# The low 16-bit step of a weight narrowing, moved from VectorE to GpSimd from tile 26 on

## The chip, the core and the metric

The kernel runs on one core of one Trainium2 chip. A core has five engines that each work through a fixed order of their own: TensorE (PE in the profile; its weight loads are PEld), VectorE (DVE), ScalarE (ACT), GpSimd (POOL) and SyncE (SP), which issues most DMA transfers. GpSimd issues some transfers too. The metric is the device time of one execution in microseconds (us), taken as the median of several runs. Of the kernel before three runs were timed: 965.84, 966.92 and 969.87 us, so the median is 966.92. A separate execution was profiled.

## The reference

Three layers follow each other. The inputs of attention are float32; the weights of the two layers behind it are float64 arrays:

```python
# 1. attention: q, k, v are (4 batches, 8 heads, 576, 64)
q_rot, k_rot = rotate(q), rotate(k)          # x1*cos - x2*sin, x1*sin + x2*cos on the two halves of 64
scores = q_rot @ k_rot.T / sqrt(64)
attn = exp(scores - max(scores)); attn /= sum(attn) + 1e-9
x = (attn @ v) as 2304 tokens x 512
# 2. moe1: w1, w2, w3 are 512x768, w_out is 768x512
h = max(x @ w1, x @ w2, x @ w3);   x = h @ w_out
# 3. moe2: w_in is 512x2048, w_out is 2048x512
h = x @ w_in;   g = h / (1 + exp(-h));   return g @ w_out     # 2304 tokens x 512, float32
```

All of it is computed in one launch.

## The kernel before

**Tiles and stages.** Attention goes batch by batch and, in a batch, by pairs of heads. A pair is cut into tiles of query rows. For each tile TensorE makes the scores (L440 and L443), VectorE takes the negated maximum (L453, output `nb`), ScalarE takes the exponential (L460, output `e`), VectorE the reciprocal of the sums (L470), and ScalarE normalises (L472). The result is moved through four DMA transfers (L511, `pt<-e`) into another layout, transposed in place by VectorE (L533, `pt<-pt`), and multiplied with v on TensorE (L574 and L578, output `xp`). VectorE or ScalarE evacuates that product (L582, L581). Between these steps TensorE works on moe1 of the batch before (L673, outputs `m`), whose results VectorE and ScalarE combine (L704, L711, L702, L727). The function `attention()` yields once per tile, and the tile's number is `j`.

**Ropes.** q and k of a pair of heads are loaded by SP into a raw buffer `qk` (L305, two transfers each for q and for k, and L308 for the last 64 rows). For batches after the first, the rotation (the rope) is done wholly by GpSimd: three instructions (L366, L367, L370) on the q half (128x512 elements), the same three on the k half (128x512), and the same three on the rest (128x128). The fourth instruction of a rope is thus the first that needs k.

**The narrowing.** The weights of moe2 lie in DRAM with 64-bit elements and are narrowed on chip to 32 bits by `narrow_w2`, in 64 pieces of 128x256, first 32 of `moe2_w_in` ("wi"), then 32 of `moe2_w_out` ("wo"). Each step `n` of that generator issues work for several pieces at once:

- the load of piece `n` into a buffer `z64` (four of them in turn): by SP for wi, by GpSimd's queue for wo (both L869)
- the cast of piece `n-2` on ScalarE, from the upper 32-bit word of each element into a buffer `z` (L229; `narrow_a` with `low=False`)
- the low step of piece `n-3` on VectorE: it writes the third 16-bit word of each element of `z64` from the second (L241; `narrow_low`)
- the second and third step of piece `n-3` on VectorE: shift and mask of `z` (L248), and the merge of `z64` into `z` (L249), which reads what the low step wrote; both are in `narrow_b`
- the measure of piece `n-5` on ScalarE (L155), and its store to a scratch in DRAM (by SP, L844, for wi; by GpSimd's queue, L849, for wo), from which it comes back later (`za<-zwi`, L976) to be summed by GpSimd (L982)

So the work on a piece is: load, cast (ScalarE), low step, second step, third step (VectorE), measure and store. A piece's `z64` is free for a new load when its third step is done.

**What sets the order.** The program is written as generators that are advanced tile by tile, and a scheduler turns it into one fixed order per engine by a simulation of the timeline; `tc.issue_after(x)` holds an instruction back until `x` has been placed. The low, second and third step are held behind the last maximum, the cast behind the last exponential. On the chip each engine takes its instructions in its fixed order and waits on semaphores for what they need.

**Where tile 26 is.** `LOOSE` is 25, and `attention()` sets `b_now[0]` to 1 for `j > LOOSE`, so from tile 26 on. The narrowing's first L248 of all starts at 176.1 us in the trace, the last third step at 535.5.

Of the kernel before, what the change touches and what calls it, by code (L numbers as in the profile page):

```python
# [12 lines left out]
ALU = mybir.AluOpType  # L13
# [9 lines left out]
def fused_kernel(  # L23
# [22 lines left out]
    nc = tc.nc  # L46
# [66 lines left out]
    ps_am, b_now = [], [0]  # L113
# [69 lines left out]
    class Weights:  # L183
# [50 lines left out]
                else:  # L234
                    nc.scalar.activation(out=q[:, :, 2], in_=q[:, :, 1], func=AF.Copy, scale=step, bias=off)

        def narrow_low(self, r):
            if r is None:
                return
            q = r.bitcast(U16).rearrange("p (n t) -> p n t", t=4)  # L240
            nc.vector.tensor_scalar(out=q[:, :, 2], in0=q[:, :, 1], scalar1=2.0 ** -13, scalar2=2.0 ** -15 - 0.5, op0=ALU.mult, op1=ALU.add)  # L241

        def narrow_b(self, i, r):
            if r is None:
# [586 lines left out]
    def narrow_w2(W, src, nm):  # L831

        part = {}
        M = W.m * 512 // 256
        for n in range(M + 5):
            if n >= 5:
                W.measure(n - 5)
                if nm == "wi":  # L840
                    i, o = divmod(n - 5, 2)
                    q, c = divmod(i, KC)
                    half, f = divmod(4 * q + 2 * o, HB)
                    nc.sync.dma_start(  # L844
                        out=zscr[nm].rearrange("p (f c a i n) -> p f c a i n", c=2, a=2, i=2, n=P)[:, f:f + 2, c % 2, c // 2, half],
                        in_=W.t[n - 5].rearrange("p (f n) -> p f n", n=P),
                    )
                else:
                    nc.gpsimd.dma_start(out=zscr[nm][:, (n - 5) * 256:(n - 4) * 256], in_=W.t[n - 5])  # L849
            if 3 <= n <= M + 2:  # L850
                with tc.issue_after(last["max"]):
                    W.narrow_low(part.get(n - 3))
                    W.narrow_b(n - 3, part.pop(n - 3, None))
            if 2 <= n <= M + 1:
                if wide:
                    W.t[n - 2] = z_p.tile([P, 256], F32, tag="z", name="z")
                with tc.issue_after(exps[-1]):
                    W.narrow_a(n - 2, part.get(n - 2), low=False)
            if n < M:
                i, o = divmod(n * 256, 512)  # L860
                if nm == "wi":
                    q, c = divmod(i, KC)
                    from_ = src[c * P:(c + 1) * P, q * 512 + o:q * 512 + o + 256]
                else:
                    from_ = src[i * P:(i + 1) * P, o:o + 256]
                if wide:
                    part[n] = z64_p.tile([P, 256], w1.dtype, tag="z64", name="z64")
                    with tc.issue_after(last["load"]) if nm == "wi" else nullcontext():
                        (nc.sync if nm == "wi" else nc.gpsimd).dma_start(out=part[n], in_=from_)  # L869
                else:  # L870
                    W.t[n] = z_p.tile([P, 256], F32, tag="z", name="z")
                    nc.sync.dma_start(out=W.t[n], in_=from_)
            yield
        t = W.scale_a(n=M)
        yield
        with tc.issue_after(last["score"]):
            W.scale_b("s" + nm, t)
        yield
# [464 lines left out]
    def narrow_all():  # L1343
        yield from narrow_w2(WI, wi2, "wi")
        yield from narrow_w2(WO, wo2, "wo")
# [118 lines left out]
```

## Time and profile before

| | us |
|---|---|
| median of three runs | 966.92 |
| profiled execution | 963.49 |
| its span | 961.7 |

| engine | busy us | share of the span |
|---|---|---|
| TensorE (PE) | 898.0 | 93% |
| its weight loads (PEld) | 666.2 | |
| VectorE (DVE) | 708.4 | 74% |
| ScalarE (ACT) | 608.4 | 63% |
| GpSimd (POOL) | 479.4 | 50% |

The span runs from the first to the last recorded instruction; 1.79 us of the execution lie around it. Busy shares are averages over stages with different limits. Idle time of an engine that is not the bottleneck costs nothing by itself, so for a change the question is which wait ends last in the stage that it touches.

### The profile page before, as it was taken

The page shows a single profiled execution, that of the slowest core. Times are in us where ns is not written, and L with a number is a line of the kernel's source. Part 1 is how long each engine was busy: PE and PEld are TensorE (multiplying, and loading weights), DVE is VectorE, ACT ScalarE, POOL GpSimd, SP SyncE. Part 2 cuts the span into 40 slices and gives each one's busy share as a digit, 9 for nine tenths or more (in the row PEclk, how much of TensorE's full clock was granted, in tenths as well). Part 3 has the DMA queues.
Part 4 walks back from the last instruction along what each step waited for, and adds up shares of the span by engine and source line. Part 5 has one row for each costly group of instructions (what it writes and reads, how often), then busy time and mean ns, then how long its engine had stood idle before and what let it go on. Part 6 is the DMA issues. An engine that isn't in the chain of part 4 may idle for free.

```text
span 961.7 us, 19066 instructions
## 1 busy us (share of the span) xinstructions
PE 898.0 (93%) x6802; PEld 666.2 (69%) x6802; DVE 708.4 (74%) x1271; ACT 608.4 (63%) x1405; POOL 479.4 (50%) x546
## 2 busy tenths in 40 slices
PE   2787998999999999999998999999998999999997
PEld 1453665656666666556655787788887888888886
DVE  6769887877788677889888577365786767766554
ACT  1988678758788677798888445453553545545342
POOL 6744585870326503543443066355485466463363
PEclk9688999999999999999999999999999999999999
DMA  6953034968899976899987852364443443423201
GB/s 153 288 148 109 14 105 124 190 122 190 184 193 202 215 140 148 228 232 230 264 232 207 211 184 88 115 198 132 132 150 102 135 157 102 138 84 131 62 1 45
DMA packets 173679, 146.30 MB, mean 152 GB/s; under 512 B 50960, under 2 KB 156176, under 8 KB 173584
## 3 DMA queue, kind: packets, MB, share of 16 engines
q1 hardware_dynamic: 167984, 131.77, 54.8%
q0 software_dynamic: 4096, 12.59, 4.2%
q8 instruction: 54, 0.88, 0.4%
q10 hardware_dynamic: 1504, 0.72, 0.3%
q14 instruction: 41, 0.34, 0.1%
HBM read 90.51 MB, written 26.21 MB: 121 GB/s over the span
## 4 chain that ended last, share of the span: by engine, by line
PE 50%; DMA 10%; DVE 9%; ACT 6%; SPq 5%; issue 4%; POOL 2%; DVEq 0%; ACTq 0%; POOLq 0%
PE m L673 9%; PE m L1114 8%; PE mb L1114 6%; DMA pt<-e 6%; PE c L1177 4%; PE a L1177 4%; PE b L1177 4%; SPq L511 3%; PE mg L673 3%; PE s L443 2%; PE xp L578 2%; PE d L1177 2%; POOL gsum L1061 2%; ACT e L472 2%; ACT e L460 1%
## 5 line engine op out<-in xcount | busy, mean ns | idle before, releaser
L673 PEld LDWEIGHTS <-w 128*128 128x128 f16 x1632 | 159.4, 98 | 59.7 <-issue 16.2
L673 PE MATMUL m<-x,w 128*128 128x256 f16 (+1 forms) x1348 | 185.3, 287 | 9.8 <-DVE t L704 4.6
L1177 PEld LDWEIGHTS <-g 128*128 128x128 f16 x1485 | 146.1, 98 | 17.7
L1114 PEld LDWEIGHTS <-w8s 128*128 128x128 f16 x1344 | 131.1, 98 | 16.1 <-issue 0.9
L460 ACT ACTIVATE e<-s,nb 128x576 f32<-128x576 f32 x144 | 105.3, 737 | 33.9 <-DVE nb L453 26.7
L453 DVE TENSOR_REDUCE nb<-s 128x2 f32<-128x1152 f32 (+1 forms) x80 | 98.4, 1231 | 32.0 <-PE s L443 26.8
L472 ACT ACTIVATE e<-e,rec 128x576 f32<-128x576 f32 x144 | 103.9, 765 | 9.4 <-DVE rec L470 8.9
L366 POOL TENSOR_TENSOR w<-qk,sin_sb 128x512 f32<-128x512 f32 (+2 forms) x40 | 42.4, 1060 | 115.1 <-DMA qk<-in_q_dram 100.4
L443 PE MATMUL s<-T 64*128 64x512 f32 x256 | 78.7, 685 | 0.0
L578 PE MATMUL xp<-pt,vd 128*64 128x256 f32 (+1 forms) x512 | 77.0, 417 | 0.2 <-DVE pt L533 0.2
L533 DVE STREAM_TRANSPOSE pt<-pt 128x1024 f32<-128x1024 f32 (+1 forms) x60 | 67.6, 1128 | 11.4 <-DMA pt<-e 11.4
L1128 POOL TENSOR_TENSOR z<-t 128x256 f32<-128x256 f32 x32 | 27.1, 847 | 89.6 <-DVE t L1120 53.9
L1066 DVE SCALAR_TENSOR_TENSOR g<-gsum,sg,g 128x1024 f16<-128x1024 f32 x36 | 49.1, 1371 | 22.1 <-ACT g L1065 21.7
L1065 ACT ACTIVATE g<-gsum,sg 128x1024 f16<-128x1024 f32 x36 | 40.8, 1141 | 37.1 <-POOL gsum L1061 37.1
L673 PE MATMUL m<-h,wo 128*128 128x256 f16 (+1 forms) x448 | 62.1, 286 | 0.4 <-POOL wo L175 0.3
L673 PEld LDWEIGHTS <-wo 128*128 128x128 f16 x512 | 49.6, 98 | 15.7 <-issue 2.0
L578 PEld LDWEIGHTS xp<-pt,vd 128*64 128x64 f32 x512 | 35.4, 137 | 33.6 <-issue 12.1
L1177 PE MATMUL c<-w,g 128*128 128x256 f16 x376 | 48.9, 277 | 0.0
L367 POOL TENSOR_TENSOR qk<-qk,cos_sb 128x512 f32<-128x512 f32 (+2 forms) x44 | 47.3, 1079 | 2.8
L1177 PE MATMUL b<-w,g 128*128 128x256 f16 x376 | 48.5, 273 | 0.0
L1177 PE MATMUL a<-w,g 128*128 128x256 f16 x376 | 47.9, 273 | 0.0
L955 POOL TENSOR_TENSOR z<-z 128x256 f32<-128x256 f32 x32 | 30.4, 978 | 32.0 <-DMA z<-zwo 26.2
(268 smaller groups left out, 1999.8 us busy)
## 6 DMA issues: line engine op xcount, KB each, us to landing
w8s<-w8scr SPq DMA_DIRECT2D x64, 448.0 KB, 4.4
pt<-e SPq DMA_DIRECT2D x192, 128.0 KB, 4.4
z<-in_moe_w_in_dram SPq DMA_DIRECT2D x32, 256.0 KB, 3.8
z<-in_moe_w_out_dram POOLq DMA_DIRECT2D x32, 256.0 KB, 4.4
w8scr<-w8o SPq DMA_DIRECT2D x32, 256.0 KB, 3.7
w<-in_moe_w_dram SPq DMA_DIRECT2D x6, 768.0 KB, 5.3
wo<-in_moe_w_dram SPq DMA_DIRECT2D x6, 768.0 KB, 4.9
qk<-in_q_dram SPq DMA_DIRECT2D x32, 128.0 KB, 3.5
```

The costliest lines, as they stand in the source:

```text
L366: tt(out=w4, in0=t4, in1=sin2, op=ALU.mult)
L367: tt(out=t4, in0=t4, in1=cos2, op=ALU.mult)
L443: last["s"] = last["score"] = nc.tensor.matmul(s[:, o:o + 512], qs[r], kt[r], start=True, stop=True).ins
L453: x = nc.vector.tensor_reduce(out=nb[:, 0:m], in_=both(s, 0, 960, 576) if m > 1 else s[:, 0:576], op=ALU.max, axis=AX.X, negate=True)
L460: x = nc.scalar.activation(out=e[:, HK[g]], in_=s[:, SK[g]], func=AF.Exp, bias=nb[:, g:g + 1], accum_out=sm[:, g:g + 1])
L472: nc.scalar.activation(out=e[:, HK[g]], in_=e[:, HK[g]], func=AF.Copy, scale=r[:, g:g + 1])
L533: nc.vector.transpose(out=x, in_=x)
L578: nc.tensor.matmul(xp[r, 0:n], v4[:, g, c, :], turned(c, g), start=False, stop=(c == 3))
L673: x = nc.tensor.matmul(ps[:, 0:n], l, r, start=(first and i == 0), stop=(not more and i == len(passes) - 1))
L1066: nc.vector.scalar_tensor_tensor(out=l, in0=x, scalar=sg_t[jb], in1=h, op0=ALU.mult, op1=ALU.subtract)
L1114: nc.tensor.matmul(o, l, r, start=(i == 0), stop=(i == len(passes) - 1))
L1177: x = nc.tensor.matmul(ps, l, r, start=first, stop=last_, skip_group_check=True)
```

## The change

The low step gets its engine as an argument. A small function `low(i, eng)` issues the low step of piece `i` once, and remembers it in the set `lows`. From tile 26 on (`b_now[0]` set), step `n` issues the low step of piece `n-2` on GpSimd, right behind ScalarE's cast of the same piece. Where it has not been issued by then, the low step of piece `n-3` is issued on VectorE ahead of the second step, as before. All else is written as it was.

```diff
-        def narrow_low(self, r):
+        def narrow_low(self, r, eng):
             if r is None:
                 return
             q = r.bitcast(U16).rearrange("p (n t) -> p n t", t=4)
-            nc.vector.tensor_scalar(out=q[:, :, 2], in0=q[:, :, 1], scalar1=2.0 ** -13, scalar2=2.0 ** -15 - 0.5, op0=ALU.mult, op1=ALU.add)
+            eng.tensor_scalar(out=q[:, :, 2], in0=q[:, :, 1], scalar1=2.0 ** -13, scalar2=2.0 ** -15 - 0.5, op0=ALU.mult, op1=ALU.add)
...
-        part = {}
+        part, lows = {}, set()
         M = W.m * 512 // 256
+
+        def low(i, eng):
+            if i not in lows:
+                lows.add(i)
+                W.narrow_low(part.get(i), eng)
+
         for n in range(M + 5):
...
             if 3 <= n <= M + 2:
                 with tc.issue_after(last["max"]):
-                    W.narrow_low(part.get(n - 3))
+                    low(n - 3, nc.vector)
                     W.narrow_b(n - 3, part.pop(n - 3, None))
...
                 with tc.issue_after(exps[-1]):
                     W.narrow_a(n - 2, part.get(n - 2), low=False)
+                if b_now[0]:
+                    low(n - 2, nc.gpsimd)
```

In the orders of the built programs, 59 of the 64 low steps stand on GpSimd and five (pieces 0 to 4) on VectorE. The number of instructions on TensorE and ScalarE is the same. From tile 26 on the scheduler's order also differs in other places. In the new program the lines behind the change have other numbers: L844, L849, L869, L976 and L982 of before are L850, L855, L877, L984 and L990. Pieces count from 0; the buffer z64_0_2974 (z64_0_2973 before) holds piece 20, z64_1_3067 piece 21, and so on up to z64_2_3405 (z64_2_3404 before) with piece 26 and z64_3_3506 with piece 27.

First place: GpSimd's order at the rope on the raw buffer qk_0_3739 (before). In the rows a name left of the arrow is written, those right of it are read.

```order
L366 TENSOR_TENSOR w_0_4063<-qk_0_3739,sin_sb_0_120 128x512
L367 TENSOR_TENSOR qk_0_3739<-qk_0_3739,cos_sb_0_119 128x512
L370 TENSOR_TENSOR qk_0_3739<-qk_0_3739,w_0_4063 128x512
L366 TENSOR_TENSOR w_0_4063<-qk_0_3739,sin_sb_0_120 128x512
L367 TENSOR_TENSOR qk_0_3739<-qk_0_3739,cos_sb_0_119 128x512
L370 TENSOR_TENSOR qk_0_3739<-qk_0_3739,w_0_4063 128x512
L366 TENSOR_TENSOR w_0_4063<-qk_0_3739,sin_sb_0_120 128x128
L367 TENSOR_TENSOR qk_0_3739<-qk_0_3739,cos_sb_0_119 128x128
L370 TENSOR_TENSOR qk_0_3739<-qk_0_3739,w_0_4063 128x128
```

And the same place now, from the rope's fourth instruction on; the raw buffer is called qk_0_3740.

```order
L366 TENSOR_TENSOR w_0_4063<-qk_0_3740,sin_sb_0_120 128x512
L241 TENSOR_SCALAR z64_0_2974<-z64_0_2974 128x256
L367 TENSOR_TENSOR qk_0_3740<-qk_0_3740,cos_sb_0_119 128x512
L370 TENSOR_TENSOR qk_0_3740<-qk_0_3740,w_0_4063 128x512
L366 TENSOR_TENSOR w_0_4063<-qk_0_3740,sin_sb_0_120 128x128
L367 TENSOR_TENSOR qk_0_3740<-qk_0_3740,cos_sb_0_119 128x128
L370 TENSOR_TENSOR qk_0_3740<-qk_0_3740,w_0_4063 128x128
L241 TENSOR_SCALAR z64_1_3067<-z64_1_3067 128x256
L241 TENSOR_SCALAR z64_2_3127<-z64_2_3127 128x256
```

The low step of piece 20 now stands behind the rope's fourth instruction, and those of pieces 21 and 22 behind the whole rope.

SP's order at the loads of that rope, before: q, then k in two transfers with the move of a tile (pt) between them.

```order
L305 DMA qk_0_3739<-in_q_dram 128x4x64 x2
L308 DMA qk_0_3739<-in_q_dram 64x2x64
L869 DMA z64_2_3126<-in_moe2_w_in_dram 128x256
L844 DMA zwi_0_137<-z_2_2971 128x2x128
L305 DMA qk_0_3739<-in_k_dram 128x4x64
L511 DMA pt_1_3107<-e_1_3024 32x8x128 x4
L305 DMA qk_0_3739<-in_k_dram 128x4x64
```

And now.

```order
L305 DMA qk_0_3740<-in_q_dram 128x4x64 x2
L308 DMA qk_0_3740<-in_q_dram 64x2x64
L877 DMA z64_2_3127<-in_moe2_w_in_dram 128x256
L850 DMA zwi_0_137<-z_2_2971 128x2x128
L305 DMA qk_0_3740<-in_k_dram 128x4x64 x2
L511 DMA pt_1_3108<-e_1_3025 32x8x128 x4
```

The second k load has moved ahead of the four pt transfers.

VectorE's order at the same place now: the third steps of pieces 20 and 21 (L249) and what stands behind them up to the maximum of the next tile.

```order
L249 SCALAR_TENSOR_TENSOR z_0_3124<-z64_0_2974,z_0_3124 128x256
L470 RECIPROCAL rec_3_3312<-rec_3_3312 128x1
L704 SCALAR_TENSOR_TENSOR t_0_3277<-m_1_3264,t_5_3262 128x256
L249 SCALAR_TENSOR_TENSOR z_1_3234<-z64_1_3067,z_1_3234 128x256
L124 TENSOR_REDUCE amax_1_3327<-tr_0_3325 1x1
L582 SCALAR_TENSOR_TENSOR x_0_2096<-xp_0_3300,vs_1_1815,x_0_2096 128x320
L453 TENSOR_REDUCE nb_0_3293<-s_0_3289 128x2
```

Each third step now waits for GpSimd; behind that of piece 21 stand a reduction of one row, an evacuation and the maximum.

Second place: GpSimd's order at the rope on qk_2_4163, which had no other work between its nine instructions before. Now:

```order
L241 TENSOR_SCALAR z64_1_3337<-z64_1_3337 128x256
L366 TENSOR_TENSOR w_0_4560<-qk_2_4163,sin_sb_0_120 128x512
L367 TENSOR_TENSOR qk_2_4163<-qk_2_4163,cos_sb_0_119 128x512
L370 TENSOR_TENSOR qk_2_4163<-qk_2_4163,w_0_4560 128x512
L366 TENSOR_TENSOR w_0_4560<-qk_2_4163,sin_sb_0_120 128x512
L241 TENSOR_SCALAR z64_2_3405<-z64_2_3405 128x256
L241 TENSOR_SCALAR z64_3_3506<-z64_3_3506 128x256
```

The low steps of pieces 26 and 27 stand behind the fourth instruction of this rope, the first that reads k.

VectorE's order at the third step of piece 26, before.

```order
L241 TENSOR_SCALAR z64_2_3404<-z64_2_3404 128x256
L248 TENSOR_SCALAR z_2_3589<-z_2_3589 128x256
L470 RECIPROCAL rec_3_3632<-rec_3_3632 128x2
L249 SCALAR_TENSOR_TENSOR z_2_3589<-z64_2_3404,z_2_3589 128x256
L453 TENSOR_REDUCE nb_0_3625<-s_0_3621 128x2
L533 STREAM_TRANSPOSE pt_0_3377<-pt_0_3377 128x1024
```

And now.

```order
L248 TENSOR_SCALAR z_2_3589<-z_2_3589 128x256
L470 RECIPROCAL rec_3_3633<-rec_3_3633 128x2
L249 SCALAR_TENSOR_TENSOR z_2_3589<-z64_2_3405,z_2_3589 128x256
L453 TENSOR_REDUCE nb_0_3626<-s_0_3622 128x2
L533 STREAM_TRANSPOSE pt_0_3378<-pt_0_3378 128x1024
```

The maximum and the transpose stand right behind the third step as before; the low step has left VectorE.

SP's order at the loads of this rope, now.

```order
L305 DMA qk_2_4163<-in_q_dram 128x4x64 x2
L308 DMA qk_2_4163<-in_q_dram 64x2x64
L305 DMA qk_2_4163<-in_k_dram 128x4x64
L511 DMA pt_1_3576<-e_0_3461 32x8x128 x4
L305 DMA qk_2_4163<-in_k_dram 128x4x64
```

Before, these rows stand in the same sequence, and the second k load is transfer 302 of SP's order in both programs, with the same 301 transfers ahead of it.

## Rows read from the trace of the kernel before

**Rows 1.** busy time by stretch: start:end, us, then per engine, TensorE clock, DMA

```profile
280.00:330.00 50.00, 49.63 (x346) 32.04 (x346) 39.74 (x80) 39.55 (x118) 32.60 (x37) 1.00 1.01 206
...
sum 370.00, PE 356.57 PEld 229.43 DVE 298.31 ACT 287.03 POOL 149.69; mean PE 118.86 PEld 76.48 DVE 99.44 ACT 95.68 POOL 49.90
```

**Rows 2.** waits, 175 to 540 us: total us, times, longest

```profile
POOL w L366 <- DMA qk<-in_q_dram: 100.4, 4, 43.6
DVE nb L453 <- PE s L443: 20.1, 16, 3.2
...
PE s L440 <- ACT e L460: 4.7, 7, 1.2
...
PE s L433 <- ACT e L460: 2.1, 3, 1.2
```

**Rows 3.** VectorE groups by form: busy us, mean ns | idle before

```profile
L249 DVE SCALAR_TENSOR_TENSOR z<-z,z 128x256 int32<-128x256 int32 x64 | 34.4, 537 | 0.4
L241 DVE TENSOR_SCALAR z<-z 128x256 uint16<-128x256 uint16 x64 | 30.2, 472 | 0.0
L248 DVE TENSOR_SCALAR z<-z 128x256 int32<-128x256 int32 x64 | 27.2, 425 | 0.0
```

**Rows 4.** VectorE's timeline, 284 to 291 us: start, us, instruction [idle before]

```profile
284.37 0.40 DVE L249 SCALAR_TENSOR_TENSOR z<-z,z 128x256 int32<-128x256 int32 x1
...
287.31 1.34 DVE L453 TENSOR_REDUCE nb<-s 128x2 f32<-128x1152 f32 x1
...
289.74 0.44 DVE L241 TENSOR_SCALAR z<-z 128x256 uint16<-128x256 uint16 x1
289.98 0.31 DVE L248 TENSOR_SCALAR z<-z 128x256 int32<-128x256 int32 x1
```

**Rows 5.** GpSimd groups by form, the same operation on wider tiles

```profile
L233 POOL TENSOR_SCALAR wo<-wo 128x768 uint16<-128x768 uint16 x6 | 12.4, 2069 | 4.6 <-ACT w L229 3.4 <-ACT rec L469 0.9
...
L233 POOL TENSOR_SCALAR w<-w 128x512 uint16<-128x512 uint16 x5 | 7.5, 1492 | 4.3 <-ACT wo L229 4.0
```

**Rows 6.** instructions of L248 and L249: least/median/most ns, first to last

```profile
L248 DVE TENSOR_SCALAR z<-z x64: 304/317/1353, 176.1 to 534.6; 128x256 int32<-128x256 int32 x64
...
L249 DVE SCALAR_TENSOR_TENSOR z<-z,z x64: 400/422/1471, 177.5 to 535.5; 128x256 int32<-128x256 int32 x64
```

**Rows 7.** GpSimd's timeline, 281 to 321 us

```profile
281.74 1.54 POOL L370 TENSOR_TENSOR qk<-qk,w 128x512 f32<-128x512 f32 x1
285.83 1.27 POOL L366 TENSOR_TENSOR w<-qk,sin_sb 128x512 f32<-128x512 f32 x1 [2.56 <-DMA zwi<-z]
...
291.47 0.46 POOL L370 TENSOR_TENSOR qk<-qk,w 128x128 f32<-128x128 f32 x1
...
320.35 1.27 POOL L366 TENSOR_TENSOR w<-qk,sin_sb 128x512 f32<-128x512 f32 x1 [0.45 <-POOL qk L370]
```

**Rows 8.** SP's timeline, loads of k

```profile
277.89 0.55 SPq L305 DMA_DIRECT2D qk<-in_k_dram  x1
...
281.63 0.61 SPq L305 DMA_DIRECT2D qk<-in_k_dram  x1
...
316.27 0.62 SPq L305 DMA_DIRECT2D qk<-in_k_dram  x1
```

**Rows 9.** TensorE's timeline at 290 us

```profile
290.30 0.49 PE L440 MATMUL s<-kd,T 128*128 128x128 f32 x2 [0.37 <-ACT e L460]
```

**Rows 10.** VectorE's timeline, 309 to 313 us

```profile
309.48 0.55 DVE L249 SCALAR_TENSOR_TENSOR z<-z,z 128x256 int32<-128x256 int32 x1
310.82 1.36 DVE L453 TENSOR_REDUCE nb<-s 128x2 f32<-128x1152 f32 x1 [0.78 <-PE s L443]
312.09 1.24 DVE L533 STREAM_TRANSPOSE pt<-pt 128x1024 f32<-128x1024 f32 x1
```

**Rows 11.** TensorE's timeline, 315 to 317 us

```profile
315.33 1.08 PE L578 MATMUL xp<-pt,vd 128*64 128x256 f32 x8
316.34 0.49 PE L440 MATMUL s<-kd,T 128*128 128x128 f32 x2
```

## The prediction

> **What bounds the kernel now.** The change acts from tile 26 to the last narrowed piece, 175 to 545 us, so I read busy time by stretch first [rows 1]. TensorE is busy for 356.57 of these 370 us: no more than 13.4 us can be won there, since nothing is taken from TensorE. From 280 to 330 it is idle for 0.37 us: in that stretch any wait that reaches it is lost time. VectorE is busy for 298.31 us and GpSimd for 149.69. Then the waits [rows 2]: VectorE's maximum waits 20.1 us for TensorE's scores, in 16 tiles, while TensorE waits only 4.7 and 2.1 us, in ten tiles, for the exponentials that stand behind that maximum. So TensorE leads and VectorE mostly follows close behind. GpSimd's ropes wait 100.4 us in just four waits for a q that has not landed. That row matters most: an instruction put behind such a rope in GpSimd's order comes late, and in the kernel before nothing with a deadline stands there.
>
> **What goes from VectorE.** 59 of the 64 low steps (the first five are issued before tile 26 and stay). Their mean is 472 ns [rows 3], 27.8 us in all. But the queue doesn't hold that long: the low step that began at 289.74 is followed at 289.98 [rows 4]. A step takes 0.24 us of VectorE's queue, 59 x 0.24 = 14.2 us.
>
> **What GpSimd takes on.** No row shows this step at 256 elements there. The same operation with the same stride took 1492 ns at 512 and 2069 ns at 768 elements [rows 5]; the line through both gives 0.92 at 256. Bounds: half of the first, 0.75, and the first itself, 1.49. I take 0.9, on the line: 53 us on an engine with 220 us free. As busy time it fits.
>
> **What the two engines do to each other.** VectorE's second step has a median of 317 ns and a maximum of 1353, its third 422 and 1471 [rows 6]; the means are 425 and 537 [rows 3]. I put this excess, 64 x (0.108 + 0.115) = 14.3 us, wholly down to GpSimd working beside, the most it can be: 0.096 us for each of its 149.7 us, and 5 us for 53 more. That leaves 14.2 - 5 = 9 us, 0.15 us per piece. The Trainium skill ("SBUF — State Buffer", section "Who interferes with whom") has a cause for such outliers: the two engines share a port pair, which one of them holds for its whole instruction against some kinds of VectorE operation. The trace agrees so far that both steps come out over 0.9 us longer at worst. Another page ("Perfetto Trace Analysis", "Optimizing Scalar/DVE Operations") warns that moving work between just these two might not help; by it the relief below would be 0 instead of -1.5 and the sum +10.5 instead of +9.
>
> **Relief on the path.** It counts only where TensorE waits for an exponential: ten gaps [rows 2] by one step each, 10 x 0.15 = 1.5 us. Bounds: 0, and 4.7 + 2.1 = 6.8 if every such wait goes. I take -1.5, since a step of 0.24 us is small beside gaps of 0.7.
>
> **The wait that is added.** The third step of a piece, on VectorE, now waits for GpSimd, and behind it on VectorE stand evictions, the reciprocal, the next maximum and the transpose that feeds TensorE's products with v. So each low step has a deadline: the start of the third step in the trace of before. Where GpSimd is idle, 0.9 us fits between cast and deadline. It doesn't at the ropes between 279 and 329 us. Pieces count from 0.
>
> First place, pieces 20 and 21. In the old trace the rope on qk_0_3739 ends its third step at 281.74 + 1.54 = 283.28 and waits for its k half until 285.83 [rows 7], whose second load was issued at 281.63 behind four pt transfers [rows 8]. In the new order that load is next to the first, issued at 277.89: it lands before 283.3, and the fourth step can start at once, 2.5 us earlier. With piece 20 between, the rope ends not at 291.47 + 0.46 = 291.9 [rows 7] but at 291.9 - 2.5 + 0.9 = 290.3. Piece 21 stands behind it and ends at 291.2; VectorE wanted it at 284.37 [rows 4]. Behind it come a short reduction, one evacuation and the maximum: about 292.4 where it was 287.31 [rows 4], 5.1 us late. Slack behind that is none: the scores of 290.30 had waited 0.37 us for the exponential [rows 9]. I'd charge 4.5 us for this place alone.
>
> Second place, piece 26. It stands behind the fourth step of the rope on qk_2_4163, which began at 320.35 [rows 7]. This step needs the second k load, issued at 316.27 [rows 8]. That load has the same place behind the same four pt transfers in SP's order in both programs, and the same transfers before it, so I see nothing that lets it land earlier. The fourth step (1.27) and piece 26 (0.9) then end at 322.5. VectorE wanted the piece at 309.48, and right behind stand the maximum (310.82) and the transpose (312.09) [rows 10]. The third step of 0.55 goes first, so the maximum starts near 323.1, 12.3 us late, and the transpose ends at 312.09 + 1.24 + 12.3 = 325.6. TensorE's products that need it began at 315.33, with the next scores behind them at 316.34 [rows 11]: 325.6 - 315.3 = 10.3 us late, less what TensorE can do meanwhile. Its order is fixed, and between the two scores it keeps the same work, so I take 10.
>
> The two places don't add: a shift of 4.5 us at the first moves VectorE's deadline at the second, while the landing of the load is held by SP's order. So 10 covers both, unless the shift holds up SP as well: the pt transfers ahead of the load need exponentials, and then the charge is 10 + 4.5 = 14.5. From below it is 0: GpSimd could be early, if that load comes well before 316.27, or TensorE could have work that I don't see. Pieces 22 to 25 lie between the places and come out late by less than 26.
>
> Behind 330 us, with the w_out pieces, GpSimd's order holds loads and sums that themselves wait for VectorE and ScalarE. There I find two or three low steps late by under 1 us, most of it covered, and take +0.5, bounds 0 and 4. Stores to DRAM and loads of weights stay on their queues; they only move with their pieces.
>
> **The sum.** -1.5 + 10 + 0.5 = +9 us. On the profiled execution, 963.49 (span 961.7 and 1.79 around it), that is 972.5. The median of the three runs, 966.92, lies 3.43 above that execution, and the forecast goes by it: 975.9 us.
>
> **Rivals.**
> - The late steps are absorbed (chance 0.20): the load for piece 26 comes early enough, or its wait is filled, and only part of the first place is left. For it: VectorE waits for TensorE longer than the other way round [rows 2]. Against: 0.37 us of idle in 50 [rows 1]. Then -1.5 + 4.5 + 0.5 = +3.5, 970.4 us, down to 966 if the first place goes too.
> - VectorE's relief counts in full (chance 0.11, the other side): all ten score waits go and no low step is late, 966.92 - 6.8 = 960.1 us. For it: the 13.4 us of idle in this stage lie to a half at these waits. Against: 0.15 us per piece, and the ropes. It decides if GpSimd is ahead of both deadlines by a step.
> - The two places add (chance 0.14): SP is held by the first, through transfers that wait for exponentials and through z64 loads that wait for VectorE's third step, and the load of piece 26 comes later too. -1.5 + 14.5 + 0.5 = +13.5, 980.4 us, and up to 984 with the upper bound of the w_out half. It decides as soon as SP has no idle time in which to catch up.
> - That the change doesn't do what it says I rule out: by the orders GpSimd holds 59 low steps and VectorE 5.
>
> **How the numbers follow.** The forecast has 0.55, its own range 971 to 979. 0.5%, 4.8 us, is about what a measurement of this kernel can tell from no change, so slower begins at 971.8: nearly all of the forecast (0.48) and all of the third case (0.14) and a little of the first, 0.63 together. Faster, under 962.1, is most of the second, 0.09. The rest is 0.28. The range runs from 963, which holds the first rival and leaves out the second, to 982, inside the third.
>
> **What would show it.** Right: 59 low steps of near 0.9 us on GpSimd; idle time of VectorE before its third step, put down to GpSimd's L241, some 5 to 7 us near 284 to 291 and more near 312 to 322; TensorE's idle time from 280 to 335 up from under 1 us to about 10, before products with v or scores, and hardly changed elsewhere. Wrong: the qk load of piece 26 issued well before 316; no wait of VectorE for L241 over 2 us; or such waits with TensorE busy through them. A low step of 0.5 us or less would leave the late places as they are, since landings set them. If TensorE's idle time from 330 to 545 falls by more than 3 us, the relief was undersized.

## The result, and the profile after

The changed kernel takes 977.75 us (median of six runs, 974.65 to 982.6), the kernel before in the same comparisons 968.06 us (six runs, 965.84 to 970.11). The ratio is 1.0105, 95% interval 1.0072 to 1.0137: slower by about 10 us. The forecast was +9 us, 975.9 us. The two profiled executions lie further apart, 977.17 against 963.49 us, and only 9 of these 13.7 us arise where the change acts, as the table below shows.

The first lines of the page after. Columns: busy us, share of the span, instructions.

```profile
span 975.4 us, 19139 instructions
...
PE 899.1 (92%) x6802; PEld 667.5 (68%) x6802; DVE 697.2 (71%) x1212; ACT 609.5 (62%) x1405; POOL 524.8 (54%) x605
```

TensorE's work is what it was (898.0 before), so the loss is idle time. VectorE has 11 us less work, GpSimd 45 us more. The groups by form, which answer to [rows 3]: busy us, mean ns of one, idle time before.

```profile
L241 POOL TENSOR_SCALAR z<-z 128x256 uint16<-128x256 uint16 x59 | 48.6, 824 | 109.7 <-ACT rec L469 57.6 <-ACT z L229 49.2
...
L249 DVE SCALAR_TENSOR_TENSOR z<-z,z 128x256 int32<-128x256 int32 x64 | 35.2, 551 | 11.3 <-POOL z L241 10.2
...
L248 DVE TENSOR_SCALAR z<-z 128x256 int32<-128x256 int32 x64 | 27.9, 436 | 0.8 <-ACT z L229 0.6
...
L241 DVE TENSOR_SCALAR z<-z 128x256 uint16<-128x256 uint16 x5 | 2.4, 478 | 0.0
```

A low step takes 0.82 us on GpSimd on average. The new number is the 10.2 us that VectorE's third step waits for it, in four waits. The waits from 175 to 340 us (total us, times, longest), for [rows 2]:

```profile
DVE z L249 <- POOL z L241: 10.1, 3, 7.8
...
PE xp L578 <- DVE pt L533: 5.9, 1, 5.9
...
PE s L440 <- ACT e L460: 3.6, 3, 1.8
...
PE tr L387 <- DVE pt L483: 2.2, 1, 2.2
```

TensorE's own gaps follow below it. Here is the chain at the second place, piece 26, engine by engine: SP's second k load (row 316.27 of [rows 8]), GpSimd's fourth rope step and the low steps, VectorE's third step with the maximum and the transpose behind it [rows 10], TensorE's last products and the product with v behind the gap [rows 11].

```profile
318.06 0.62 SPq L305 DMA_DIRECT2D qk<-in_k_dram  x1
```

```profile
322.92 1.26 POOL L366 TENSOR_TENSOR w<-qk,sin_sb 128x512 f32<-128x512 f32 x1 [1.89 <-DMA pt<-e]
324.27 1.83 POOL L241 TENSOR_SCALAR z<-z 128x256 uint16<-128x256 uint16 x2
```

```profile
325.06 0.42 DVE L249 SCALAR_TENSOR_TENSOR z<-z,z 128x256 int32<-128x256 int32 x1 [7.78 <-POOL z L241]
325.40 1.35 DVE L453 TENSOR_REDUCE nb<-s 128x2 f32<-128x1152 f32 x1
326.67 1.23 DVE L533 STREAM_TRANSPOSE pt<-pt 128x1024 f32<-128x1024 f32 x1
```

```profile
320.19 1.91 PE L673 MATMUL m<-h,wo 128*128 128x256 f16 x16
327.96 2.40 PE L578 MATMUL xp<-pt,vd 128*64 128x256 f32 x10 [5.86 <-DVE pt L533]
```

Read from the top: the load is issued at 318.06, GpSimd idles until it has landed, the low step queued behind runs at 324.27, VectorE has stood for 7.78 us, and TensorE for 5.86 us. The releaser that is named at 322.92 is a pt transfer, the one that ended last by the records, but the fourth step reads k. The view of this load (KB, us from issue to landing), first in the changed kernel, then before, shows that k fits:

```profile
qk<-in_k_dram SPq DMA_DIRECT2D x1, 128.0 KB, 4.7
```

```profile
qk<-in_k_dram SPq DMA_DIRECT2D x1, 128.0 KB, 4.0
```

318.06 + 4.7 = 322.8, and the step starts at 322.92; before, 316.27 + 4.0 = 320.3, and it started at 320.35 [rows 7]. At the first place the chain is there too, but short:

```profile
291.30 0.42 DVE L249 SCALAR_TENSOR_TENSOR z<-z,z 128x256 int32<-128x256 int32 x1 [1.87 <-POOL z L241]
...
293.24 1.35 DVE L453 TENSOR_REDUCE nb<-s 128x2 f32<-128x1152 f32 x1
```

```profile
274.65 0.49 PE L440 MATMUL s<-kd,T 128*128 128x128 f32 x2 [1.81 <-ACT e L460]
...
281.37 0.63 PE L387 MATMUL tr<-ident,qk 128*128 128x128 f32 x4 [2.19 <-DVE pt L483]
...
296.23 0.49 PE L440 MATMUL s<-kd,T 128*128 128x128 f32 x2 [1.41 <-ACT e L460]
```

The gap of 1.41 us stands behind the first place, but little of it is owed to the low step: run e2 below, in which no low step is late, has 1.15 us there. The two gaps before it, at tiles 38 and 39, wait for no low step: they come with TensorE's changed order.

How the delay builds up: the start of each tile's maximum, less its start before, less the same difference at tile 24 (up to where the programs agree; the two executions already differed by 2.07 us there). Each column is one profiled execution; the labels are those of the experiments below.

| tile (its start before) | changed | e5 | e2 | e4 | e11 |
|---|---|---|---|---|---|
| 38 (273.5) | 1.4 | 1.5 | 1.4 | 0.2 | 0.2 |
| 39 (278.2) | 4.8 | 5.1 | 5.3 | 0.0 | 0.2 |
| 41 (291.9) | 3.9 | 7.4 | 4.1 | 0.6 | 4.5 |
| 43 (304.8) | 6.2 | 10.6 | 6.6 | 0.2 | 5.0 |
| 44 (310.8) | 12.5 | 10.7 | 7.8 | -0.1 | 11.6 |
| 48 (337.9) | 10.9 | 8.2 | 4.7 | -0.2 | 9.8 |
| 55 (380.4) | 11.3 | 8.6 | 5.1 | -0.3 | 10.3 |
| 79 (530.6) | 9.0 | 6.2 | 3.6 | -3.7 | 10.5 |

In the changed kernel 3.4 us come at tile 39, 6.3 at tile 44, and some 3.5 are given back later. From tile 79 to the end the profiled pair drifts apart by another 2.6 us, where the two programs do the same work; with the 2.07 us at the start that makes 13.7.

### The profile page after: what moved, and what is told of

It is laid out like the page before. It is cut to its first block, busy times and chain, and to the rows that moved or that the text cites. A ratio compares the mean times of both kernels' runs of the same rounds, so it can differ in the third digit from the quotient of the medians.

```text
span 975.4 us, 19139 instructions
## 1 busy us (share of the span) xinstructions
PE 899.1 (92%) x6802; PEld 667.5 (68%) x6802; DVE 697.2 (71%) x1212; ACT 609.5 (62%) x1405; POOL 524.8 (54%) x605
## 5 line engine op out<-in xcount | busy, mean ns | idle before, releaser
L241 POOL TENSOR_SCALAR z<-z 128x256 uint16<-128x256 uint16 x59 | 48.6, 824 | 109.7 <-ACT rec L469 57.6
L578 PEld LDWEIGHTS xp<-pt,vd 128*64 128x64 f32 x512 | 36.3, 139 | 40.3 <-issue 12.3
```

The source lines that it names most:

```text
L241: eng.tensor_scalar(out=q[:, :, 2], in0=q[:, :, 1], scalar1=2.0 ** -13, scalar2=2.0 ** -15 - 0.5, op0=ALU.mult, op1=ALU.add)
L578: nc.tensor.matmul(xp[r, 0:n], v4[:, g, c, :], turned(c, g), start=False, stop=(c == 3))
```

## The experiments

Theory A is that of the prediction: low steps that come late behind a rope make VectorE, and then TensorE, wait. Rival B is that GpSimd's extra work slows VectorE by itself. Rival C is that the changed order on TensorE and SP costs by itself. Ratios are to the kernel before, with 95% intervals.

**e4, nobody waits.** The low step's output goes to the lowest 16-bit word, which no instruction reads.

```diff
-                    low(n - 2, nc.gpsimd)
+                    lows.add(n - 2)
+                    q = part[n - 2].bitcast(U16).rearrange("p (n t) -> p n t", t=4)
+                    nc.gpsimd.tensor_scalar(out=q[:, :, 0], in0=q[:, :, 1], scalar1=2.0 ** -13, scalar2=2.0 ** -15 - 0.5, op0=ALU.mult, op1=ALU.add)
```

Expected: 

> Leaves out: the low step itself. From tile 26 on GpSimd does the same operation at the same places, but writes the lowest 16-bit word, which nobody reads, so VectorE's third step waits for nothing; the engines' orders are those of the changed kernel but for a few rows. Theory A (low steps that come late behind a rope make VectorE and then TensorE wait): the 5.86 us gap of TensorE before a product with v is gone, ratio to before about 0.999 to 1.002 (967 to 970 us). Rival B (GpSimd's extra 49 us of work slow VectorE down by themselves): the work is the same, the ratio stays near 1.010. Rival C (the changed order on TensorE and SP costs by itself, 4.8 us of shift between tiles 33 and 39): ratio 1.004 or more, with the gaps of 1.8 and 2.2 us before tiles 38 and 39 still there.

Measured: 0.9984 (0.9969 to 0.9998), -1.5 us. TensorE's waits from 240 to 345 us:

```profile
PE xp L578 <- DVE pt L533: 0.7, 1, 0.7
```

GpSimd does as much as in the changed kernel (47.2 us of such steps against 48.6) and the loss is gone, which rules out B. C is not ruled out: 117 rows of TensorE's order differ from the changed kernel, and among them are those before tiles 38 and 39, where both gaps are missing here. So the orders are not quite as alike as the expectation says.

**e5, pieces 26 and 27 back on VectorE.**

```diff
-                if b_now[0]:
+                if b_now[0] and not (nm == "wi" and 26 <= n - 2 <= 27):
```

Expected: 

> The changed kernel, but pieces 26 and 27 keep their low step on VectorE; the orders are otherwise the same within some ten rows. Theory A: VectorE's wait of 7.8 us and TensorE's gap of 5.86 us near 322 us are gone, the shift of 6.3 us between tiles 43 and 44 with them; ratio 1.003 to 1.005 (971 to 973 us). Rivals B and C: 57 of 59 low steps and nearly all of the order stay, ratio within 0.001 of 1.0105.

Measured: 1.0071 (1.0048 to 1.0093). A third of the loss goes, less than expected, and as the two intervals overlap even that is not clear of noise. The gap near 322 us is gone, but another has grown:

```profile
297.48 0.80 PE L440 MATMUL s<-kd,T 128*128 128x128 f32 x2 [4.10 <-ACT e L460]
```

That is the first place, 1.41 us in the changed kernel. Here q and k landed later (GpSimd began the rope at 280.24 instead of 279.54, and its fourth step at 284.97 instead of 283.66), and VectorE waited longer for piece 21:

```profile
292.55 0.42 DVE L249 SCALAR_TENSOR_TENSOR z<-z,z 128x256 int32<-128x256 int32 x1 [3.22 <-POOL z L241]
```

This place comes earlier in time than the one that the edit takes away, and up to 340 us SP and TensorE have the same order in both kernels. So what the first place costs differed between two executions by the landings ahead of it; why they came later here is not shown.

**e2, pieces 20 to 27 back on VectorE** (the same edit with 20 for 26).

Expected: 

> The changed kernel, but pieces 20 to 27 (all that stand at the three ropes from 279 to 330 us) keep their low step on VectorE; 51 stay on GpSimd. Theory A: both late places are gone, ratio 0.999 to 1.002. Rival B: 51 of 59 parts of the loss stay, ratio 1.009. Rival C: TensorE's order is close to that of the changed kernel, ratio 1.004 to 1.006.

Measured: 1.0039 (1.0021 to 1.0056). TensorE's order up to 340 us is that of the changed kernel but for a few products, and VectorE waits 0.2 us for low steps in the whole stage:

```profile
L249 DVE SCALAR_TENSOR_TENSOR z<-z,z 128x256 int32<-128x256 int32 x64 | 38.6, 605 | 1.2 <-POOL z L241 0.2
```

So removing the late low steps takes 0.66%, 6.4 us, off the changed kernel, and what is left, 0.39% or 3.8 us, is no wait for GpSimd:

```profile
277.24 0.49 PE L440 MATMUL s<-kd,T 128*128 128x128 f32 x2 [1.81 <-ACT e L460]
284.43 0.63 PE L387 MATMUL tr<-ident,qk 128*128 128x128 f32 x4 [1.03 <-DVE pt L483]
299.04 0.49 PE L440 MATMUL s<-kd,T 128*128 128x128 f32 x2 [1.15 <-ACT e L460]
```

The gap of 1.81 us stands at the same place in all kernels that share this order of TensorE (the changed one, e2 and e5): there three products of moe1 stand between two scores, some 24 in the kernel before, so the exponential between them is not covered. That is rival C, for its part. The 3.8 us are put down to it with the relief already taken off; no run changes TensorE's order alone.

**e11, pieces 12 to 19 back on VectorE.**

```diff
-                if b_now[0]:
+                if b_now[0] and not (nm == "wi" and 12 <= n - 2 <= 19):
```

Expected: 

> The changed kernel with pieces 12 to 19 back on VectorE. TensorE's order is then that of before up to tile 39 or so, while pieces 20 to 63 still stand on GpSimd among the ropes: piece 26 now behind the first step of the rope on qk_2_4163 (q) instead of the fourth (k). If C is the main cause: the gaps of 1.8 and 2.2 us are gone and the ratio is 0.998 to 1.000. If A is: VectorE still waits for pieces 20, 21 and 26 (the latter until about 318 us, 8 us late), ratio 1.003 to 1.008.

Measured: 1.0102 (1.0074 to 1.0130), above what either theory gave. TensorE's order is that of before up to the first place (293 us) and differs from both kernels behind it, the gaps of 1.81 and 2.19 us are gone, and the loss is whole: 4.3 us at the first place (tiles 39 to 41 of the table), 6.6 us at the second. At the first, VectorE waited for piece 21:

```profile
291.01 0.42 DVE L249 SCALAR_TENSOR_TENSOR z<-z,z 128x256 int32<-128x256 int32 x1 [4.37 <-POOL z L241]
```

At the second, GpSimd stood before the first step of the rope instead of the fourth, waiting for q:

```profile
321.69 1.26 POOL L366 TENSOR_TENSOR w<-qk,sin_sb 128x512 f32<-128x512 f32 x1 [2.60 <-DMA qk<-in_q_dram]
323.03 1.83 POOL L241 TENSOR_SCALAR z<-z 128x256 uint16<-128x256 uint16 x2
```

```profile
323.82 0.43 DVE L249 SCALAR_TENSOR_TENSOR z<-z,z 128x256 int32<-128x256 int32 x1 [7.84 <-DMA z<-in_moe_w_in_dram]
```

```profile
326.72 1.98 PE L578 MATMUL xp<-pt,vd 128*64 128x256 f32 x8 [5.61 <-DVE pt L533]
```

(VectorE's releaser is put down to a load here; that load's data had been cast at 315, and the third step began 0.8 us behind the start of the two low steps, the length of the first.) So A needs no C. In the changed kernel the two causes overlap: of what comes late at tile 39 (4.8 us) little is lost again at the first place (6.2 at tile 43). It need not be so: in e5 the same rows go from 5.1 to 10.6 us.

**e7, each low step twice.** The second does the same again.

```diff
                 if b_now[0]:
                     low(n - 2, nc.gpsimd)
+                    W.narrow_low(part.get(n - 2), nc.gpsimd)
```

Expected: 

> Each low step is done twice on GpSimd, the second time with the same result, so GpSimd has 49 us more work than in the changed kernel and a low step takes 1.6 us. A: what makes the steps late is the landing of q and k ahead of them, so each late place grows by 0.8 us or so, ratio 1.011 to 1.015. B: the loss doubles, ratio 1.02.

Measured: 1.0107 (1.0080 to 1.0133), as much as the changed kernel and just under what A gave. The groups:

```profile
L241 POOL TENSOR_SCALAR z<-z 128x256 uint16<-128x256 uint16 x118 | 95.8, 812 | 78.6 <-ACT rec L469 44.1 <-ACT z L229 26.4
...
L249 DVE SCALAR_TENSOR_TENSOR z<-z,z 128x256 int32<-128x256 int32 x64 | 33.8, 530 | 22.0 <-POOL z L241 20.6 <-DMA z<-in_moe_w_in_dram 0.8
...
L248 DVE TENSOR_SCALAR z<-z 128x256 int32<-128x256 int32 x64 | 28.7, 449 | 0.6 <-ACT z L229 0.5
```

With 95.8 us of low steps VectorE's second and third steps take 62.5 us, with 48.6 us 63.1, with none on GpSimd 61.6 [rows 3]; in e4, with 47.2 us, they take 57.9. B is out: the work doubles, and neither these steps nor the loss grow with it. What a late place pays for a longer low step the run does not show, since its orders are others: the maximum and the transpose that stood behind piece 26 stand ahead of its third step, the gap of 5.86 us is missing, VectorE waits 14 times instead of four, and TensorE's gaps from 262 to 345 us are these:

```profile
277.52 0.49 PE L440 MATMUL s<-kd,T 128*128 128x128 f32 x2 [3.86 <-DVE z L249]
302.56 0.80 PE L440 MATMUL s<-kd,T 128*128 128x128 f32 x2 [5.36 <-ACT e L460]
```

**e3, no low step at all** (from piece 5 on), `lows.add(n - 2)` in place of the call.

Expected: 

> Leaves out: the low step of pieces 5 to 63, on every engine. It shows VectorE's relief alone. Theory A: relief of 1.5 us, ratio 0.998 (0.993 if all score waits go), and the difference to the run in which GpSimd works for nobody is the price of GpSimd's work beside VectorE, under 3 us. Rival B: that difference is 8 us or more. The order of the engines differs widely from both kernels here, so 3 us either way can be due to that.

Measured: 0.9960 (0.9943 to 0.9976), -3.9 us: a relief shows and is small, though the orders differ here too. The difference to e4 is 2.3 us, within the 3 us that the expectation left to the differing orders, so it does not price GpSimd's work.

**e1 and e6, one half of the pieces only.** `if b_now[0] and nm == "wo"`, and with "wi".

Expected: 

> GpSimd takes the low step of the 32 w_out pieces only; up to tile 54 the orders are those of before. Theory A with C (the loss lies at late low steps between tiles 39 and 44 and in TensorE's changed order there; behind tile 55 the changed kernel gains 2.3 us): no loss, ratio 0.996 to 0.999 (963 to 966 us). Rival B (loss in proportion to GpSimd's extra work, 32 of 59): 1.0055.

Expected: 

> GpSimd takes the low step of the w_in pieces 5 to 31 only. A with C: the loss of the changed kernel without the gain behind tile 55, ratio 1.011 to 1.014. B (27 of 59): 1.005. TensorE's gaps before tiles 38 and 39 (1.8 and about 2 us) and the one before a product with v near 322 us are there.

Measured: w_out alone 1.0026 (1.0000 to 1.0052), w_in alone 1.0106 (1.0082 to 1.0130). The whole loss is in the w_in half. I had expected the w_out half to gain 2 to 3 us; it doesn't. In its profile 2.04 us go at 340.7, before scores whose order is that of before and where the kernel before has a gap of 0.94 us, and 2.8 are won back behind tile 55. What makes its runs spread from 964.15 to 974.66 us stays open.

**e14 and e10, what stands at no rope of 242 to 330 us:** `nm == "wi" and n - 2 < 12`, and that with `nm == "wo"`.

Expected: 

> GpSimd takes the low step of pieces 5 to 11 only, which are done before 242 us; TensorE's order is that of before. A: no late step, no relief that reaches TensorE (it is idle for under 1 us from 205 to 280), ratio 0.999 to 1.001. B (7 of 59): 1.001.

Expected: 

> GpSimd takes the low step of pieces 5 to 11 and of the 32 w_out pieces, so none that stands at the ropes between 242 and 330 us. This is the best guess at a version that keeps the relief without the late steps: A gives 0.997 to 1.001; as the run with the w_out half alone gave 1.0026 (1.0000 to 1.0052), 1.002 would say that the w_out half brings no relief either.

Measured: 1.0010 (0.9989 to 1.0031) and 1.0019 (0.9998 to 1.0040). Neither can be told from the kernel before; none of the versions that do the low step on GpSimd beats it. The gap that e1 has at 340.7 us is 3.01 us in e10, and the exponential ahead of it waits for a pt transfer and for no low step (2.71 us in the kernel before):

```profile
336.44 0.74 ACT L460 ACTIVATE e<-s,nb 128x576 f32<-128x576 f32 x1 [4.79 <-DMA pt<-e]
```

Why that transfer lands later stays open.

**e12 and e13, ropes that wait for nothing.** In the ropes of batches 2 and 3 the three operations leave out the rotation: they read the sine and cosine tables and write the scratch.

```diff
+            if free:
+                tt(out=w4, in0=cos2, in1=sin2, op=ALU.mult)
+                tt(out=w4, in0=w4, in1=cos2, op=ALU.mult)
+                x = tt(out=w4, in0=w4, in1=sin2, op=ALU.add)
+                continue
```

Expected: 

> The kernel before, but the ropes of batches 2 and 3 leave out the rotation: GpSimd does the same number of operations of the same shapes on tables that lie on the chip, and waits for no q or k. TensorE's order is that of before. All theories: as before, ratio 0.998 to 1.001. It is the base for the next run.

Expected: 

> The changed kernel, all 59 low steps on GpSimd, with the ropes of batches 2 and 3 as in the run before this one (the rotation left out, no wait for q or k; the same operations). Theory A (low steps wait behind ropes whose q or k has not landed): VectorE waits under 1 us for a low step, no gap of TensorE over 2 us between 285 and 325 us, ratio 0.996 to 1.000. Rivals B (GpSimd's work slows VectorE) and C (the order costs by itself): the ratio stays at 1.004 or more.

Measured: 1.0069 (1.0041 to 1.0096) for the base and 1.0093 (1.0064 to 1.0122) with the change. The base was to be as before and is not, so only the two against each other speak: 976.33 to 974.44 us, +0.2%, where the real ropes give +1.05%. From 279 to 330 us VectorE waits for no low step. But it isn't the clean test that I wanted: the ropes now run in one dense row, and low steps behind them make VectorE wait 11.0 us in five waits before and after that stretch (3.5 us near 273, for example).

## Why the prediction was right

- **The second place: right, place and path.** The load that the low step waits for was issued at 318.06 us (316.27 before), not earlier; the maximum started at 325.4 (forecast 323.1), the transpose ended at 327.9 (325.6), and TensorE's gap is before the product with v that needs it. Less the 2.07 us by which the two executions already differed, these are 323.3 and 325.8, and the product is 327.96 - 2.07 - 315.33 = 10.6 us late, where 10 was forecast. The gap is 5.86 us and not 10, since TensorE was already 4.7 us late when it fell idle (320.19 + 1.91 = 322.10). Its idle time from 280 to 335 us rises from 0.4 to 8.6 us, where about 10 was forecast.
- **"The two places don't add": right.** TensorE came to the second place 4.7 us late and left it 10.6 us late, not 14.5: the landing sets it. In e11 the delay at tile 44 is 11.6 us against 12.5, but there it is the landing of q, so that the two lie so close shows nothing more.
- **The first place: right as a mechanism, wrong for the changed kernel.** I charged 4.5 us there alone. With before's order, in e11, it is 4.3 us. In the changed kernel VectorE waits 1.87 us instead of 5 to 7, and TensorE's gap there is only some 0.3 us longer than without late low steps (1.41 against 1.15). The tiles were already 4.8 us late, which can hide part of it, but that is not the whole reason: in e5 they were 5.1 us late, and VectorE waited 3.22 us.
- **What I missed: TensorE's order.** I compared the scores near piece 26 and took the order between them as kept; the sum has no term for a changed order, and TensorE's idle time was to be hardly changed elsewhere. Five tiles earlier it had changed, and 3.4 us were lost at tile 39. Without late low steps 0.39% is left, with the relief taken off (e2); the late low steps cost the other 0.66%.
- **What is luck.** That the second place still ends 10.6 us late is not: the landing absorbs what was lost before. But the clock behind the gap (1.6 us, last section) and the 3.5 us given back between tiles 44 and 79 are in no term of the sum, and that they partly cancel is luck.
- **Relief on the path: agrees, not shown.** Forecast -1.5 us, e4 -1.5 (0.9984, interval 0.9969 to 0.9998). But e4 and e3 (-3.9) have other orders than the changed kernel, and e10 and e14, with no late low step, show no relief.
- **GpSimd's low step:** forecast 0.9 us, measured 0.82. **Slowing of VectorE's steps:** forecast 5 us, measured 1.5 (63.1 against 61.6), and with 57.9 in e4 for nearly the same work no slowing is shown. Both forecasts were too high; the late places, set by landings, do not turn on them.
- **The w_out half:** forecast +0.5 us; e6 has the whole loss without it, and e1 gives 1.0026 with an interval from 1.0000. Not settled closer.
- **The rivals.** Absorbed waits (970.4 us) and relief in full (960.1) did not come about. The rival in which both places add (980.4) needs SP to fall behind. It issued the load 1.8 us later than before, less than the 2.07 us by which the executions already differed: it did not fall behind.

## What to carry to other kernels

Before a short step goes to an engine with time to spare, look at what stands ahead of it in that engine's order and what that waits for: 0.8 us behind a rope whose k had not landed held VectorE for 7.8 us. Compare the time at which the step can run at the earliest there with the time at which its reader ran before; that difference was forecast at 12.3 us for the maximum at the second place and came to 12.5. At the first place it was near (4.5 against 4.3 us) only where TensorE's order had been kept. And compare the bounding engine's order over the whole stage, not only where the new wait stands.

## What the runs showed of the hardware that was not expected

**An idle gap costs TensorE's clock as well.** Behind the gap of 5.86 us the granted clock is at half, 1.2 instead of 2.4 GHz, for some 3 us. Windows of the changed kernel: start:end, us, then busy us of each engine, the clock, DMA share, GB/s.

```profile
300.00:322.00 22.00, 22.00 (x169) 15.91 (x167) 13.08 (x30) 15.05 (x44) 17.20 (x22) 1.00 0.98 193
322.00:326.00 4.00, 0.10 (x1) 0.00 (x0) 0.94 (x2) 0.42 (x3) 2.92 (x3) 0.79 0.69 225
326.00:328.00 2.00, 0.04 (x2) 0.05 (x2) 2.00 (x3) 1.46 (x5) 1.84 (x3) 0.50 0.59 160
328.00:330.00 2.00, 2.00 (x10) 1.19 (x12) 1.60 (x3) 1.48 (x7) 1.78 (x3) 0.50 1.01 235
330.00:332.00 2.00, 2.00 (x10) 0.97 (x8) 0.00 (x0) 1.85 (x5) 1.22 (x2) 0.72 0.88 184
332.00:335.00 3.00, 3.00 (x18) 1.47 (x17) 2.04 (x2) 1.28 (x4) 0.00 (x0) 1.00 0.50 161
```

From 328 to 332 us TensorE is busy throughout, 2 us of it at 0.50 and 2 at 0.72: at full clock that work would take 2 x 0.50 + 2 x 0.72 = 2.4 us instead of 4. That is an estimate of 1.6 us that the prediction did not price. The clock is at 0.50 behind the gap of 4.10 us in e5 as well (297 to 303 us) and behind that of 5.61 us in e11 (326.7 to 330.7), and it stays at 1.00 around the gaps of 2.2 us or less in the changed kernel (270 to 300 us).

**GpSimd's low steps cost VectorE little; beside dense ropes single instructions take far longer.** In e12 GpSimd is busy for 37.18 of the 40 us from 204 to 244 (6.04 in the kernel before), and VectorE's instructions there take over three times their median at worst (0.44 us for L241, 0.48 for L716):

```profile
217.20 1.51 DVE L241 TENSOR_SCALAR z<-z 128x256 uint16<-128x256 uint16 x1
...
220.15 1.55 DVE L716 TENSOR_TENSOR h<-t,h 128x320 f16<-128x320 f32 x1
```

The delay at tile 33 (243.7 us before) is 8.6 us there. The Trainium skill ("SBUF — State Buffer", "Who interferes with whom") has VectorE's operations with two SBUF inputs contend with a GpSimd instruction that reads SBUF. L716 has two such inputs and the ropes read SBUF, so its 1.55 us agrees with that; L241 has one, and no row says what holds it. The low step reads SBUF as well, and 48.6 us of it beside VectorE show 1.5 us at most in L248 and L249. That the ropes alone make the free-rope base slower was not tested by itself.
